# The gates of a gated recurrence: fewer passes over the squares, and all work in a new order

## The chip, the core and the metric

The kernel runs on one core of a Trainium2 chip. The metric is the device time of one execution in microseconds; the kernel before was timed three times, and the median counts. One further execution was recorded by the hardware profiler; all views of the profile are of that one. The engines are called TensorE (PE, with its weight loads as PEld), VectorE (DVE), ScalarE (ACT), GpSimd (POOL) and SyncE (SP, which only issues DMAs here).

## What is computed

A gated linear recurrence with complex gates over 768 steps, for 4 batches, 8 heads and a head size of 48, and behind it a low-rank token mixer with a two-layer network of channels (384 to 1536 to 384). Cut to what matters:

```python
mag = sqrt(a_re * a_re + a_im * a_im)
scale = minimum(mag, 0.999) / (mag + 1e-06)
a_re_n, a_im_n = a_re * scale, a_im * scale
for t in range(S):
    new_re = ar * S_re - ai * S_im
    new_im = ar * S_im + ai * S_re
    S_re, S_im = new_re + outer(k[t], v[t]), new_im
    y[t] = q[t] @ S_re

xt = x.transpose(0, 2, 1)                 # x: the y of all heads side by side
u = x + (xt @ U @ V).transpose(0, 2, 1)
out = u + maximum(u @ w_ch1, 0.0) @ w_ch2
```

All arrays are fp32 in effect; the weights of the mixer come as 64-bit floats and are converted in the kernel. The real parts of the gates lie between 0.85 and 0.95, the imaginary parts are normal with a spread of 0.1.

## The kernel before, in words

The tokens are cut into 24 chunks of 128 (six per batch), and two neighbouring chunks make a gate group, so there are 12 groups. Group 0 is worked on as two halves of one chunk each.

**Gates (the function `gates`).** The recurrence is not run step by step. The kernel takes the logarithm of each gate's magnitude and its angle, sums both along the chunk with a matmul against a triangular matrix, and uses the exponentials and the cosines and sines of these sums as weights of q and k. For that, `magnitudes_of` computes per group, on tiles of 128 tokens x 768 values (two chunks of 384):

- ScalarE squares both parts in one step of 1536 values, into the planes x and y.
- VectorE adds the squares and clips the sum into l (L655), puts the larger of the squares into x (L656), and runs two range tests on the parts themselves (L658), which tell whether the imaginary part anywhere exceeds the real part. Each test writes the maximum that it found into a column of the tile `bad` (an accumulator read).
- ScalarE takes Ln of l, then Exp with a scale of -0.5 and the bias log(1e-6) into y, then Ln(1 + y): this is the log of (mag + 1e-6)/mag.
- The clip at 0.999 is a step on VectorE in groups 0 to 2 (`SPREAD`, L666) and a Relu on ScalarE in the others. A VectorE step then completes the log of the gate in l (L445 in groups 0 to 2, L671 in the others). From group 3 on (`SPLIT`) l is split into two parts for faster matmuls (L677, L678).
- ScalarE takes Ln and Exp (scale -0.5) of x, which gives one over the larger part; VectorE multiplies it by the imaginary part. The arc tangent of that is the angle; it is taken later, under another activation table.

`within` sums l along the chunk (L692, L696) and takes the exponentials; `angles` and `waves` do the same for the angle. All activations are issued through the helper in L439.

**Chunks (`prep`, `chain`).** VectorE weighs q and k (L442), TensorE transposes them (L817), ScalarE copies the result (L823), and the matmuls of the chunk follow (L846, L866, L895, L903), with the state carried from chunk to chunk.

**Mixer (`mixer`).** For every two chunks there are the products with the weights: `up` (L992) and a corrected form of it for the first two chunks (L1032, with VectorE's L1038), `few` (L1104) and `down` (L1236). From mixer 2 on `few` does a Strassen-like scheme with 15 products, and from mixer 1 on `down_two` does a similar one; for that, differences of blocks of w2 are computed once (L617, L1306). The weights arrive as raw words over the SP queue and are converted by VectorE and ScalarE (L583 to L589).

**The order.** Every operation is registered with a planner (`Plan.add`) with its engine, an estimated cost, and what it reads and writes. The program is then emitted in the order of a fixed list, `ORDER`, of 2210 numbers. Each engine and each DMA queue executes its own part of the list strictly in order. `SPARE` says before which TensorE operations a number of idle 128x128 matmuls are put, to fill a wait.

**The check at the end (`judge`).** The columns of `bad` and the smallest of the exponentials are tested and counted. If anything is out of range, a general, step-by-step path (`in_general`) computes the whole result again.

## Time and profile before

| | |
|---|---|
| runs | 559.97, 560.68, 565.65 us |
| median | 560.68 us |
| span of the profiled execution | 559.4 us |
| ACT_TABLE_LOAD | 24, 30.8 us in all |
| HBM read and written | 33.60 MB and 4.76 MB |

The span runs from the first to the last instruction of the profiled execution; the times of the runs also hold what lies around it. The profiled execution's own time is its span and that frame; the runs stand between 0.6 and 6.2 us above the span, the median 1.3.

In a row of a group of instructions stand the line, the engine, the operation, the tiles written and read, the shape, the count, then the busy time, the mean duration in ns, and after the second bar the idle time of the engine just before these instructions with what ended it. In a row of waits stand the waiting engine with its tile and line, what it waited for, the sum in us, the number and the longest. In a row of a stretch of time stand its bounds and length, then the busy time of PE, PEld, DVE, ACT and POOL with the number of instructions, the granted TensorE clock as a share of full speed, the share of the 16 DMA engines, and GB/s. Line numbers are those of the kernel before; a line can be that of a helper through which many operations go, as L439 (activations), L442 (multiplications) and L445 (additions).

### The profile page before, as it was taken

The page shows a single profiled execution, that of the slowest core. Times are in us where ns is not written, and L with a number is a line of the kernel's source. Part 1 is how long each engine was busy: PE and PEld are TensorE (multiplying, and loading weights), DVE is VectorE, ACT ScalarE, POOL GpSimd, SP SyncE. Part 2 cuts the span into 40 slices and gives each one's busy share as a digit, 9 for nine tenths or more (in the row PEclk, how much of TensorE's full clock was granted, in tenths as well). Part 3 has the DMA queues.
Part 4 walks back from the last instruction along what each step waited for, and adds up shares of the span by engine and source line. Part 5 has one row for each costly group of instructions (what it writes and reads, how often), then busy time and mean ns, then how long its engine had stood idle before and what let it go on. Part 6 is the DMA issues. An engine that isn't in the chain of part 4 may idle for free.

```text
span 559.4 us, 16683 instructions
## 1 busy us (share of the span) xinstructions
PE 533.3 (95%) x7242; PEld 481.8 (86%) x7242; DVE 432.3 (77%) x828; ACT 317.7 (57%) x553; POOL 32.2 (6%) x61
## 2 busy tenths in 40 slices
PE   2899999989999999999999999999999999999996
PEld 1677786867799997999999997899999989999996
DVE  6999989899799998898896976977572726728352
ACT  6889999894657869576567855861323322111110
POOL 1000000000011000101001001001000000000000
PEclk9999999989999999999999999999999999999999
DMA  9969876331333254133342235020011000000001
GB/s 222 198 145 201 195 182 184 91 52 37 85 66 80 45 107 76 37 69 65 60 91 51 57 52 110 16 40 27 9 36 36 4 2 22 8 8 22 21 9 33
DMA packets 150687, 39.90 MB, mean 71 GB/s; under 512 B 145912, under 2 KB 147408, under 8 KB 150608
## 3 DMA queue, kind: packets, MB, share of 16 engines
q1 hardware_dynamic: 148400, 34.43, 31.2%
q0 software_dynamic: 2208, 4.35, 2.3%
q8 instruction: 58, 0.95, 0.7%
q14 instruction: 21, 0.17, 0.1%
HBM read 33.60 MB, written 4.76 MB: 69 GB/s over the span
## 4 chain that ended last, share of the span: by engine, by line
PE 53%; DVE 20%; issue 7%; ACT 4%; DMA 3%; POOL 0%; SPq 0%; DVEq 0%; ACTq 0%; POOLq 0%
PE down L1236 20%; PE few L1104 17%; PE dk L866 3%; PE tr L817 3%; ACT gate L439 2%; DMA gate<-F 2%; PE inner L846 2%; DVE xo L445 2%; PE y L903 2%; DVE QKC L442 2%; PE up L992 1%; DVE qk L442 1%; PE y L895 1%; DVE GS L751 1%; DVE GL L671 1%
## 5 line engine op out<-in xcount | busy, mean ns | idle before, releaser
L1112 ACT COPY h<-few 128x512 f32<-128x512 f32 x60 | 34.8, 584 | 86.0 <-PE few L1104 84.6
L439 ACT ACTIVATE gate<-gate 128x768 f32<-128x768 f32 (+2 forms) x74 | 65.9, 901 | 16.6 <-DVE GS L751 9.0
L1236 PE MATMUL down<-w,h 128*128 128x192 f32 x396 | 72.7, 330 | 0.2 <-DVE xo L445 0.2
L1236 PEld LDWEIGHTS down<-w,h 128*128 128x128 f32 x396 | 64.5, 190 | 2.7 <-DVE xo L445 1.1
L445 DVE TENSOR_TENSOR xo<-down,xo 128x192 f32<-128x192 f32 (+1 forms) x79 | 29.8, 386 | 41.9 <-PE down L1236 39.7
L823 ACT COPY QK<-tr 112x512 f32<-112x512 f32 x96 | 50.0, 596 | 20.3 <-PE tr L817 20.1
L1104 PE MATMUL few<-extra,w 128*128 128x128 f32 x400 | 50.2, 276 | 0.1
L1104 PEld LDWEIGHTS few<-extra,w 128*128 128x128 f32 x400 | 47.6, 192 | 0.7 <-PE mixed L961 0.4
L1116 DVE CUSTOM_DVE_ANT_1 h<-few,h 128x512 f32<-128x512 f32 x60 | 40.2, 686 | 8.1 <-PE few L1104 4.3
L442 DVE TENSOR_TENSOR QKC<-qk,cs 128x768 f32<-128x768 f32 x48 | 44.5, 952 | 0.8 <-PE tr L817 0.6
L445 DVE TENSOR_TENSOR h<-few,h 128x512 f32<-128x512 f32 x30 | 20.5, 687 | 23.8 <-PE few L1104 12.6
L1236 PE MATMUL down<-stage 128*128 128x192 f32 x198 | 38.0, 329 | 0.5 <-DVE xo L445 0.5
L1180 POOL DMA_DIRECT2D out_dram<-xo x32 | 18.1, 573 | 276.8 <-DVE xo L445 248.5
L1236 PEld LDWEIGHTS down<-stage 128*128 128x128 f32 x198 | 32.6, 190 | 1.7 <-DVE xo L445 1.4
L992 PE MATMUL up<-uT,w 128*128 128x256 f32 x144 | 32.4, 382 | 0.2 <-ACT uT L981 0.2
L1104 PE MATMUL few<-gate,w 128*128 128x128 f32 x240 | 31.8, 277 | 0.1
L817 PEld LDWEIGHTS tr<-ident,QKC 64*112 64x112 f32 x768 | 25.2, 135 | 7.5 <-DVE QKC L442 2.5
L436 ACT ACT_TABLE_LOAD x24 | 30.8, 1283 | 1.1 <-PEq L1440 0.7
L817 PE MATMUL tr<-ident,QKC 64*112 64x64 f32 x768 | 29.8, 226 | 1.4 <-DVE QKC L442 1.4
L992 PEld LDWEIGHTS up<-uT,w 128*128 128x128 f32 x144 | 27.0, 190 | 4.4 <-ACT uT L981 0.6
L1104 PEld LDWEIGHTS few<-gate,w 128*128 128x128 f32 x240 | 29.1, 192 | 0.3 <-PE few L1104 0.2
L439 ACT ACTIVATE cs<-F 128x384 f32<-128x384 f32 x48 | 24.1, 520 | 8.1 <-DVE F L765 7.9
(161 smaller groups left out, 1106.2 us busy)
## 6 DMA issues: line engine op xcount, KB each, us to landing
stage<-in_moe_w_ch_dram SPq DMA_DIRECT2D x12, 768.0 KB, 5.4
gate<-in_a_im_dram SPq DMA_DIRECT2D x24, 192.0 KB, 3.0
gate<-in_a_re_dram SPq DMA_DIRECT2D x24, 192.0 KB, 3.7
qk<-in_q_dram SPq DMA_DIRECT2D x24, 192.0 KB, 4.4
qk<-in_k_dram SPq DMA_DIRECT2D x24, 192.0 KB, 3.6
VP<-in_v_dram SPq DMA_DIRECT2D x24, 192.0 KB, 3.9
out_dram<-xo POOLq DMA_DIRECT2D x12, 192.0 KB, 2.2
out_dram<-xo POOLq DMA_DIRECT2D x20, 96.0 KB, 1.9
```

The lines of the kernel that those rows point to most:

```text
L436: ACT(1.37, rank, lambda: nc.scalar.preload_act_table_set(name), writes=[TABLE])
L439: return nc.scalar.activation(out=o, in_=i, func=f, **kw)
L442: nc.vector.tensor_tensor(out=o, in0=a, in1=b, op=OP.mult)
L445: nc.vector.tensor_tensor(out=o, in0=a, in1=b, op=OP.add)
L817: nc.tensor.transpose(out=get(*ps[r])[0:DQ, h], in_=get(*qkc)[at, h].rearrange("p u d -> p (u d)")[:, 0:DQ], identity=ident[at, at], tile_ ...
L823: nc.scalar.copy(out=get(*QK)[:, u].rearrange("p (h t) -> p h t", t=CH)[:, :, r * HC:(r + 1) * HC], in_=get(*ps[r])[0:DQ])
L992: nc.tensor.matmul(out=get(*ps)[:, e], lhsT=w1[:, f, (ff + e) * 128:(ff + e + 1) * 128], rhs=get(*uT)[:, f], start=(f == 0), stop=(f == KD ...
L1104: nc.tensor.matmul(out=get(*ps)[:, q], lhsT=w()[:, q * 128:(q + 1) * 128], rhs=v[0](), start=(n == 0 and q == 0), stop=True, skip_group_ch ...
L1112: ACT(c_act(n3 * CH) - 0.045, RU, lambda i=i, k=k: nc.scalar.copy(out=at(i, k), in_=get(*ps)), [ps], [o])
L1116: DVE(c_dve(n3 * CH), RU, lambda i=i, k=k: nc.vector._custom_dve(dve_ops.TENSOR_ADD_SAT, out=at(i, k), in0=get(*ps), in1=at(i, k), s0=math ...
L1180: queue.dma_start(out=out[b, c * CH:(c + 1) * CH, lo:hi], in_=get("xo", i)[:, lo:hi])
L1236: nc.tensor.matmul(out=get(*to)[:, part], lhsT=x(j), rhs=y[:, j], start=(first and j == 0), stop=(j == KH - 1), skip_group_check=not first)
```

## The change

1. ScalarE squares only the imaginary part, into y. The square of the real part is a VectorE step, max(a_re, 0) * a_re, into x.
2. The two range tests become one: max(y, 1e-30) >= x, counted into one column of `bad`.
3. The clipped sum of the squares goes into y in place, behind the test, which reads y before.
4. x now holds the square of the real part and no maximum, so the step of L656 goes. In groups 1 to 11 x and y lie side by side, and one Ln and one Exp of 1536 values each serve both. In group 0 they stay apart.
5. The factor 1e-6 moves from the bias of Exp to the scale of the next Ln. The clip step reads y and writes l, ahead of the Exp that overwrites y.
6. The product that reads a changed block of w2 now names that block's change as something it reads (`turned w2`), which the planner did not know before.
7. `ORDER` is another list, of 2175 numbers, and `SPARE` another table. Per group 1 to 11 three operations are gone, and one per half of group 0.

The operations of TensorE are the same 624 in number; the idle matmuls are 33 where they were 41. The core of the diff:

```diff
 ORDER = (
-    95, 93, 91, 94, 0, 92, 150, 5, 11, 96, 99, 149, 100, 152, 97, 3, 151, 4, 98, 101, 194, 115, 112, 2, 116, 102, 195, 113, 106, 104, 196, 117, 114,
...
+    0, 95, 91, 93, 96, 97, 98, 99, 94, 92, 5, 100, 101, 112, 111, 102, 103, 105, 106, 113, 114, 115, 104, 3, 190, 108, 7, 120, 116, 6, 8, 117, 11,
...
 SPARE = {
-    125: 2, 135: 9, 184: 1, 199: 21, 203: 1, 223: 2, 250: 3, 412: 2,
+    123: 2, 133: 5, 194: 8, 198: 11, 218: 6, 248: 1,
 }
...
-            def squares():
-                at, n = slice((lo - first) * DM, (hi - first) * DM), 4 if g < SINGLE and g % 2 else 2
-                act(GATE[:, 0:2, at], GATE[:, n:n + 2, at], AF.Square)
-            ACT(c_act(2 * W), R1, squares, AR + AI, [X] + Y)
-            DVE(cd, R1, lambda: nc.vector._custom_dve(dve_ops.TENSOR_ADD_SAT, out=t(l), in0=t(x), in1=t(y), s0=M2HI, s1=M2LO), [X] + Y, [L])
-            DVE(cd, R1, lambda: nc.vector.scalar_tensor_tensor(out=t(x), in0=t(x), scalar=M2LO, in1=t(y), op0=OP.max, op1=OP.max), Y, [X])
-            for u, o in enumerate((dve_ops.TENSOR_TENSOR_REDUCE_SUB_MAX, dve_ops.TENSOR_TENSOR_REDUCE_ADD_MAX)):
-                DVE(cd + 0.06, ("least", g), lambda u=u, o=o: nc.vector._custom_dve(
-                    o, out=low[:, 0:W], in0=t(ai), in1=t(ar), s0=-math.inf, s1=1.0 - 2.0 * u,
-                    accum_out=bad[:, 1 + 2 * lo + u:2 + 2 * lo + u]), AR + AI, [("low", 0), ("bad", 0, (lo, u))])
-            table(ca, R1, lambda: act(t(l), t(l), AF.Ln), [], [L])
-            table(ca + 0.09, R1, lambda: act(t(y), t(l), AF.Exp, scale=-0.5, bias=leps), [L], Y)
-            table(ca, R1, lambda: act(t(y), t(y), AF.Ln, bias=1.0), [], Y)
+            both = g > 0
+            def pair():
+                return GATE[:, 0:2, (lo - first) * DM:(hi - first) * DM]
+            ACT(ca, R1, lambda: act(t(y), t(ai), AF.Square), AI, Y)
+            DVE(cd, R1, lambda: nc.vector.scalar_tensor_tensor(out=t(x), in0=t(ar), scalar=0.0, in1=t(ar), op0=OP.max, op1=OP.mult), AR, [X])
+            DVE(cd + 0.06, R1, lambda: nc.vector.scalar_tensor_tensor(
+                out=low[:, 0:W], in0=t(y), scalar=M2LO, in1=t(x), op0=OP.max, op1=OP.is_ge, accum_out=bad[:, 1 + lo:2 + lo]),
+                Y + [X], [("low", 0), ("bad", 0, lo)])
+            DVE(cd, R1, lambda: nc.vector._custom_dve(dve_ops.TENSOR_ADD_SAT, out=t(y), in0=t(x), in1=t(y), s0=M2HI, s1=M2LO), [X], Y)
+            if both:
+                table(c_act(2 * W), R1, lambda: act(pair(), pair(), AF.Ln), [], [X] + Y)
+            else:
+                table(ca, R1, lambda: act(t(y), t(y), AF.Ln), [], Y)
             if on_dve:
-                DVE(c_one(W), R1, lambda: nc.vector.tensor_scalar(out=t(l), in0=t(l), scalar1=-0.5, scalar2=-LNMAX, op0=OP.mult, op1=OP.max), [], [L])
+                DVE(c_one(W), R1, lambda: nc.vector.tensor_scalar(out=t(l), in0=t(y), scalar1=-0.5, scalar2=-LNMAX, op0=OP.mult, op1=OP.max), Y, [L])
+            else:
+                ACT(ca + 0.09, R1, lambda: act(t(l), t(y), AF.Relu, scale=-0.5, bias=lmax), Y, [L])
+            if both:
+                table(c_act(2 * W), R1, lambda: act(pair(), pair(), AF.Exp, scale=-0.5), [], [X] + Y)
+            else:
+                table(ca, R1, lambda: act(t(y), t(y), AF.Exp, scale=-0.5), [], Y)
+            table(ca, R1, lambda: act(t(y), t(y), AF.Ln, scale=1e-6, bias=1.0), [], Y)
...
-            table(ca, R1, lambda: act(t(x), t(x), AF.Ln), [], [X])
-            table(ca, R1, lambda: act(t(x), t(x), AF.Exp, scale=-0.5), [], [X])
+            if not both:
+                table(ca, R1, lambda: act(t(x), t(x), AF.Ln), [], [X])
+                table(ca, R1, lambda: act(t(x), t(x), AF.Exp, scale=-0.5), [], [X])
             DVE(cd, R1, lambda: mul(t(x), t(x), t(ai)), AI, [X])
...
-            product(one, 0, lambda j: of(0, 1)[:, j], w2_of(0, 1), names, first=False)
+            product(one, 0, lambda j: of(0, 1)[:, j], w2_of(0, 1), lambda half: names(half) + [("turned w2", 0)], first=False)
...
-                                                                    op=OP.subtract), [("w2s", 0)], ALL_W2)
+                                                                    op=OP.subtract), [("w2s", 0)], ALL_W2 + [("turned w2", 0)])
```

## The prediction

> **What bounds the kernel now.** I read the page first, for the engines' shares and the clock.

> ```profile
> span 559.4 us, 16683 instructions
> ...
> PE 533.3 (95%) x7242; PEld 481.8 (86%) x7242; DVE 432.3 (77%) x828; ACT 317.7 (57%) x553; POOL 32.2 (6%) x61
> ...
> PEclk9999999989999999999999999999999999999999
> ```

> TensorE is busy for 95% of the span, but a matmul's end is modelled, so a waiting TensorE can look busy; the weight loads (PEld) tell more. The one slice with a lower digit in PEclk comes back below. Next I asked for busy time by stage, because shares over the whole span mix stages with different limits.

> ```profile
> 0.00:20.00 20.00, 7.54 (x31) 5.29 (x32) 14.66 (x38) 13.00 (x23) 2.30 (x14) 1.00 1.02 211
> 20.00:140.00 120.00, 113.82 (x1719) 88.67 (x1719) 111.98 (x183) 103.78 (x174) 2.47 (x3) 0.97 0.66 140
> 140.00:340.00 200.00, 199.34 (x2925) 184.99 (x2923) 177.37 (x338) 138.47 (x237) 16.70 (x26) 1.00 0.35 68
> 340.00:360.00 20.00, 18.27 (x475) 15.20 (x474) 14.10 (x28) 15.90 (x31) 0.97 (x2) 1.00 0.31 67
> ```

> The columns are length, PE, PEld, DVE, ACT, POOL, clock, DMA share, GB/s. There are two regimes. From 140 us on TensorE is the bound: it is idle 0.66 us in 200, and weight loads fill 185 of those 200. Before 140 us they fill 88.7 of 120, while VectorE fills 112 and ScalarE 104. In the middle of that stretch VectorE has no gap at all:

> ```profile
> 40.00:60.00 20.00, 19.38 (x283) 14.68 (x284) 20.00 (x32) 17.64 (x32) 0.00 (x0) 1.00 1.04 198
> ```

> So up to 140 us the pace is set by two elementwise queues that are nearly full, and after it by TensorE. The waits tell whether it is the queues' amount of work or the latency of a chain:

> ```profile
> PE es ps L696 <- DVE GL L445: 11.1, 1, 11.1
> ...
> DVE GL L671 <- ACT GL L439: 3.6, 1, 3.6
> ...
> PE up L1032 <- DVE extra L1038: 1.9, 2, 1.0
> ```

> The first row is TensorE's wait for the first gates at the start. The second is the longest wait of VectorE between 20 and 140 us, and the third the longest sum of TensorE there. Only once in 120 us did a gate's chain leave VectorE idle for long. The chain of waits shows the same (start, length, piece):

> ```profile
> 85.04 0.87 DVE GL L671
> ...
> 106.03 0.89 DVE w L589
> 106.91 0.88 DVE GL L655
> 107.81 0.84 ACT GL L439
> ...
> 140.60 0.97 DVE GL L655
> ...
> 317.59 0.96 DVE GL L671
> ```

> At 106.03 the gates' saturating sum (L655) stands behind a weight conversion on the same queue, not behind its own inputs. L655 at 106.91 is that of group 4 and at 140.60 that of group 5, so the gates of groups 0 to 4 lie before 140 us and seven groups after it. L671, the step that completes the log of a gate, stands in the chain five times, of which the first and the last are shown.

> **The change part by part.** The prices are means of the groups by form, 128x768 for groups 1 to 11 and 128x384 for each of the two halves of group 0:

> ```profile
> L658 DVE CUSTOM_DVE_ANT_0 low<-gate 128x768 f32<-128x768 f32 x22 | 20.9, 952 | 0.8 <-DMA gate<-in_a_im_dram 0.7
> ...
> L656 DVE SCALAR_TENSOR_TENSOR gate<-gate 128x768 f32<-128x768 f32 x11 | 10.4, 950 | 0.1
> ...
> L671 DVE SCALAR_TENSOR_TENSOR GL<-GL,gate 128x768 f32<-128x768 f32 x9 | 8.6, 956 | 5.3 <-ACT GL L439 4.3 <-ACT gate L439 1.0
> ...
> L658 DVE CUSTOM_DVE_ANT_0 low<-gate 128x384 f32<-128x384 f32 x4 | 2.2, 559 | 2.9 <-DMA gate<-in_a_re_dram 2.8
> L658 DVE DVE_READ_ACCUMULATOR2_ANT bad<- 128x1 f32 x26 | 2.2, 83 | 0.0
> ```

> VectorE, per group: before, the sum (L655), the maximum (L656) and two range tests (L658), each with an accumulator read of 83 ns. After, the square of the real part, one range test with one read, and the sum. One operation of 0.952 and one read of 0.083 go: 1.035 us. The square and the sum take the place of the maximum and the sum at the same size, with two fp32 operands as L656 has. In group 0 each half saves 0.559 + 0.083, together 1.28 us.

> ```profile
> L439 ACT ACTIVATE gate<-gate 128x768 f32<-128x768 f32 x55 | 45.7, 840 | 4.9 <-DMA gate<-in_a_re_dram 2.9 <-DVE gate L656 1.7
> ...
> L439 ACT ACTIVATE gate<-gate 128x1536 f32<-128x1536 f32 x11 | 16.4, 1487 | 11.7 <-DVE GS L751 9.0 <-issue 1.4 <-ACT xo L912 0.8
> ...
> L439 ACT ACTIVATE gate<-GL,leps 128x768 f32<-128x768 f32 x11 | 10.2, 930 | 1.1 <-DVE gate L656 1.1
> L439 ACT ACTIVATE GL<-GL 128x768 f32<-128x768 f32 x11 | 9.3, 844 | 3.4 <-DVE GL L655 3.2
> L439 ACT ACTIVATE GL<-GL,lmax 128x768 f32<-128x768 f32 x9 | 8.4, 933 | 0.0
> ...
> L439 ACT ACTIVATE gate<-gate 128x384 f32<-128x384 f32 x8 | 3.8, 512 | 0.0
> ...
> L439 ACT ACTIVATE gate<-GL,leps 128x384 f32<-128x384 f32 x2 | 1.2, 599 | 0.0
> L439 ACT ACTIVATE GL<-GL 128x384 f32<-128x384 f32 x2 | 1.0, 514 | 0.0
> ```

> ScalarE, groups 1 to 11: before, both squares in one step (1.487), Ln (0.844), Exp with a bias tile (0.930) and three more steps (3 x 0.840): 5.78 us. After, one square (0.840), Ln and Exp of both planes (2 x 1.487, the price of the 1536 form, whatever the function) and one Ln (0.840): 4.65 us. That saves 1.13 us. A half of group 0 goes from 0.840 + 0.514 + 0.599 + 3 x 0.512 = 3.49 to 6 x 0.512 = 3.07, so 0.84 us for both. The Relu (0.933) and the table loads stay.

> The only operation with no row is the range test as a plain scalar-tensor-tensor with an accumulator. Its nearest rows are the same operation without one (0.950) and the custom operation with one (0.952 + 0.083). I take 0.95 + 0.083. Less is excluded, since every two-operand fp32 step of this size lies at 0.95 or above; as the upper bound I take a second pass over the data for the accumulation, 0.95 us more per group and 0.56 per half. [...]

> Sum for the first regime: VectorE loses 1.28 + 4 x 1.035 = 5.4 us by 140 us, ScalarE 0.84 + 4 x 1.13 = 5.4. Both queues shrink alike, so neither takes over from the other, and what is late next is TensorE. I pass all 5.4 us on, since VectorE's 8 idle us in that stretch come from waits that the change leaves in place. TensorE can take it: it is idle 120 - 113.82 = 6.2 us there, and more is hidden in stretched matmuls. If TensorE's order left no room, nothing of it would pass.

> Second regime: seven groups save 7.2 us of VectorE and 7.9 of ScalarE, but TensorE's idle time is only 0.66 + 1.73 = 2.4 us between 140 and 360 us. I take 0.9 of it, between nothing and 2.4.

> The start: the new list puts the load of the prefix matrix ahead of the first gate loads on SP's queue, where it stood behind three of them.

> ```profile
> 0.73 0.44 SPq L542 DMA_DIRECT2D gate<-in_a_im_dram  x1
> ...
> 2.75 0.71 SPq L531 DMA_DIRECT2D prefix_z<-in_spans_dram  x1
> ```

> One issue of 0.71 us is thus moved ahead of everything. The first matmul waits 11.1 us on that path, so it costs between 0, if landing and not issue sets the data's time, and 0.7; I take 0.3. The fillers before waiting matmuls go from 41 to 33; they stand in waits and I give them nothing. In groups 0 to 2 the clipping step on VectorE now reads the plane that the next Exp overwrites, so that Exp waits for VectorE.

> ```profile
> L666 DVE TENSOR_SCALAR GL<-GL 128x384 f32<-128x384 f32 (+1 forms) x4 | 1.8, 454 | 0.0
> ```

> Four such steps take 1.8 us. Queued behind the Exp on ScalarE are the copies of transposed q and k; the new list puts four of those between the two steps of group 1 and a square or a log between those of each half of group 0, and they cover it. Uncovered it costs those 1.8 us. The added dependency of the w2 difference only restrains the planner and costs nothing. The remaining moves of the new list I can't price one by one; I allow 2.5 us either way.

> Together: -5.4 - 0.9 + 0.3 = -6.0 us on the span of 559.4, so 553.4. The runs are 559.97, 560.68 and 565.65; the median is 1.3 above the profiled span, which gives **554.7 us**, 552 to 557.5 with the allowance.

> **Rivals.** First, more gain: the half clock goes away.

> ```profile
> 120.32 1.93 PE L1032 MATMUL up<-V,more 32*128 32x256 f32 x6 [0.91 <-DVE extra L1038]
> ...
> 120.00:127.50 7.50, 6.98 (x120) 5.74 (x122) 7.50 (x10) 6.43 (x11) 0.77 (x1) 0.54 0.54 83
> ```

> Just before 120.32 us TensorE waits 0.91 us for L1038, half of its sum there, and in the 7.5 us from 120 on its clock is 0.54: 3.4 us of clock are lost. If a shorter VectorE queue ends these waits sooner, that comes on top: 551.3 us. [...]

> Second, no measurable change: the saved work leaves idle queues. For it: the DMA share is 1.02 and 1.04 up to 60 us, so loads may set the early pace, and only groups after that (two of the five before 140 us) would pay: about -2 us, 558.5. A range test with a second pass gives the same end: 2 x 0.56 + 4 x 0.95 = 4.9 us return and 559.6 is left. Against the loads: VectorE is busy 20.00 of 20 at 40 to 60 us, so data are there. Against the second pass: the custom step accumulates too, reads two planes too and takes 0.952. I give the loads 0.11 and the second pass 0.06.

> Third, **slower**: the chain of one gate gets longer and becomes the pace. Before: squares 1.487, sum 0.950, Ln 0.844, Exp 0.930, Ln 0.840, Relu 0.933, L671 0.956, together 6.9 us. After: square on VectorE 0.95, test 1.03 (it reads the plane that the sum overwrites, so it comes first), sum 0.95, Ln of both 1.487, Relu 0.933, Exp of both 1.487, Ln 0.840, L671 0.956, together 8.6: 1.7 us more. If L671 stands in the chain five times for its latency, and the shorter queues just idle, that is +8.5: 569 us. It decides from four such groups on (6.8 us). For it: the five rows of L671. Against it: the single wait of 3.6 us for ScalarE, and pieces like 106.03, where the queue ahead is what is late.

> Fourth, the test raises its flag and the general path runs: 768 steps of some ten operations on 576 elements, at about 0.7 us by L656's row, over 5 ms. The inputs speak against it: real parts from 0.85 to 0.95, imaginary parts with a spread of 0.1.

> **How the numbers follow.** Forecast 0.55, clock gain 0.15, no change 0.17 (0.11 and 0.06), slower 0.12, flag 0.01. About 1% is what a measurement of this kernel tells from none, so the edges are 555.1 and 566.3. The forecast's own range lies a little more than half below 555.1: 0.30 faster, 0.25 within. So faster 0.30 + 0.15 = 0.45, the same 0.25 + 0.17 = 0.42, slower 0.13. The range has to hold the clock gain and the unchanged case and reach some way to the slower one: 550 to 562.5.

> **What would show it.** Right: VectorE's sum falls by about 12.7 us and ScalarE's by 13 (5.4 + 7.2 and 5.4 + 7.9), the test has 950 ns a piece, five groups' gates are done by 135 us, and the weight loads' share of the first 135 us rises. The clock gain shows as a window without 0.54. Wrong: a test near 1.9 us; a wait of VectorE or TensorE for ScalarE's gates of more than 1 us in several groups; a first matmul later than 11.1 us; or a stage after 140 us in which TensorE idles more than 2.4 us, which would be the new order's doing.

## The result: slower by 0.85%, and the profile after

The changed kernel takes 566.34 us (median of 10 runs, 565.73 to 568.82). The kernel before, on the same chip, takes 561.03 us; one of its ten executions took 2982.67 us and is left out of the ratio. The ratio is 1.0085, with a 95% interval of 1.0062 to 1.0107. 554.7 us had been forecast. The profiled run took 567.48 us; its span is 565.6 us, 6.2 more than before, where the forecast had 6.0 less. From the page of the changed kernel:

```profile
span 565.6 us, 16573 instructions
PE 529.8 (94%) x7226; PEld 479.8 (85%) x7226; DVE 427.8 (76%) x801; ACT 309.7 (55%) x531; POOL 31.7 (6%) x61
...
PEclk9999999999999989999999999999999999999997
```

The page counts work that overlaps on one engine once. Added up record by record, VectorE went from 486.5 to 474.1 us and ScalarE from 350.8 to 337.5: 12.4 and 13.3 us less. So the work did go. The slice of PEclk with an 8 has moved from the ninth to the fifteenth, and a 7 stands in the last. Busy time by stage (length, PE, PEld, DVE, ACT, POOL, clock, DMA share, GB/s):

```profile
20.00:140.00 120.00, 113.75 (x1656) 87.04 (x1657) 110.82 (x168) 103.82 (x165) 2.47 (x3) 1.00 0.62 139
140.00:340.00 200.00, 196.21 (x3136) 183.40 (x3132) 169.90 (x317) 131.36 (x226) 14.71 (x23) 0.99 0.36 67
340.00:360.00 20.00, 19.81 (x307) 18.87 (x304) 15.32 (x35) 8.54 (x16) 2.73 (x4) 1.00 0.43 77
...
120.00:127.50 7.50, 7.50 (x134) 5.45 (x133) 6.34 (x11) 4.76 (x8) 0.41 (x1) 1.00 0.57 110
200.00:210.00 10.00, 8.68 (x246) 7.94 (x242) 7.95 (x13) 6.73 (x8) 0.00 (x0) 0.83 0.62 95
```

Up to 140 us TensorE is as busy as before (113.75 against 113.82). Between 140 and 340 us it idles 3.79 us, where it idled 0.66. The half clock at 120 to 127.5 us (0.50 for 6.83 us) is gone, and another one stands at 200 to 210 us (0.50 for 3.41 us). TensorE's waits, and those of SP's queue at the end:

```profile
PE es ps L702 <- DVE GL L443: 10.4, 1, 10.4
...
PE y L901 <- ACT GL L437: 1.3, 1, 1.3
```

```profile
SPq L1457 <- PEq L1457: 6.6, 2, 6.1
```

The first matmul comes at 10.4 us (11.1 before). The last row is new: in the closing barrier SP waits 6.1 us in one piece; before, its longest wait there was 1.3 us. The chain of waits ends like this (start, length, piece):

```profile
548.63 6.13 PE down L1242 x36
554.77 0.02 issue
554.79 0.36 DVE xo L443
555.15 0.07 DVE bad L1375
555.22 0.04 issue
555.26 0.20 PE bad ps L1382 x2
555.47 0.02 issue
555.49 0.14 DVE flag L1384
```

The last product ends at 554.75 us, against 554.51 before. The loss is behind it. In the list of before, the six steps of `judge` stand at places 1495 to 1890 of 2210, and the flag is written at 438.19 us. In the new list three of the six are the last three entries, and the flag is written at 555.63 us. Every engine reads the flag (L1402) before the branch (L1412), so GpSimd begins its closing steps only then. The records of GpSimd's own queue show start and length:

```
          before          after
flag      438.06 0.14     555.49 0.14
TENSOR_LOAD   542.50 0.49     555.67 0.69
INC_SWDGE_SEM 544.61 1.12     556.93 1.12
DRAIN         548.31 3.97     560.74 3.97
end of span   559.4           565.6
```

Before, these 10 us lay beneath TensorE's last matmuls. Now they lie behind them.

To see where the 6.2 us arose, I added up TensorE's steps of each list at the length that they have without a wait, and looked when each kernel has done the same sum. The lists differ in order, so equal sums are not the same steps, and single rows are good to some half a microsecond:

```
sum done, us      0     80     90    150    170    300    340    440   last matmul   span
before         11.1  113.9  129.8  192.7  213.6  348.2  391.2  494.3     554.5     559.4
after          10.4  114.0  125.0  189.7  215.3  347.9  388.6  493.2     555.5     565.6
judge early    10.6  114.5  125.5  190.1  216.0  348.5  389.2  494.1     555.9     561.1
short test      9.7  114.1  125.1  188.2  212.3  344.8  385.6  490.2     552.1     557.2
test twice     11.8  118.7  129.6  195.1  218.7  353.3  395.1  500.0     561.8     566.7
new in old     11.6  121.7  138.6  204.5  225.3  362.5  407.5  510.9     571.1     575.9
y later        10.5  113.9  125.4  190.1  213.5  346.1  386.8  491.8     553.6     558.4
```

The lower rows are experiments, told below. For the change: nothing is gained by 114 us and 4.8 us by 130, across the half clock of before. Of these 1.8 are gone by 190 us, and 4.7 more are lost by 214, where the wait of 1.3 us and the half clock lie. By 494 us TensorE is 1.1 us ahead again (before waits 1.6 us at 348), and at its last matmul, which is now the count's, it is 0.95 us late (0.24 at the last product). The other 5.2 us are the tail.

### The profile page after: what moved, and what is told of

It is laid out like the page before. It is cut to its first block, busy times and chain, and to the rows that moved or that the text cites. A ratio compares the mean times of both kernels' runs of the same rounds, so it can differ in the third digit from the quotient of the medians.

```text
span 565.6 us, 16573 instructions
## 1 busy us (share of the span) xinstructions
PE 529.8 (94%) x7226; PEld 479.8 (85%) x7226; DVE 427.8 (76%) x801; ACT 309.7 (55%) x531; POOL 31.7 (6%) x61
## 4 chain that ended last, share of the span: by engine, by line
PE 62%; DVE 15%; issue 10%; ACT 5%; DMA 3%; SPq 3%; POOL 0%; DVEq 0%; POOLq 0%; ACTq 0%
PE down L1242 22%; PE few L1110 21%; PE y L909 3%; PE tr L823 3%; PE inner L852 2%; ACT gate L437 2%; PE dk L872 2%; DMA gate<-F 2%; DVE QKC L440 2%; SPq L540 2%; PE y L901 2%; PE up L998 2%; PE uTp L983 1%; DVE xo L443 1%; PE mixed L967 1%
## 5 line engine op out<-in xcount | busy, mean ns | idle before, releaser
L437 ACT ACTIVATE gate<-gate 128x768 f32<-128x768 f32 (+2 forms) x78 | 75.1, 968 | 29.7 <-DVE gate L658 15.7
L1242 PE MATMUL down<-w,h 128*128 128x192 f32 x396 | 70.9, 328 | 1.1 <-DVE xo L443 1.0
L1110 PE MATMUL few<-extra,w 128*128 128x128 f32 x400 | 52.5, 278 | 1.0 <-DVE GM L443 0.8
L443 DVE TENSOR_TENSOR xo<-down,xo 128x192 f32<-128x192 f32 (+1 forms) x79 | 30.1, 385 | 29.1 <-PE down L1242 29.1
L1122 DVE CUSTOM_DVE_ANT_1 h<-few,h 128x512 f32<-128x512 f32 x60 | 39.8, 686 | 13.3 <-PE few L1110 9.1
L443 DVE TENSOR_TENSOR h<-few,h 128x512 f32<-128x512 f32 x30 | 20.5, 688 | 31.1 <-PE few L1110 15.9
L998 PE MATMUL up<-uT,w 128*128 128x256 f32 x144 | 34.2, 386 | 1.6 <-ACT h L437 1.2
L437 ACT ACTIVATE es<-es ps 128x384 f32<-128x384 f32 x48 | 21.1, 494 | 21.4 <-PE es ps L698 20.4
L1110 PE MATMUL few<-gate,w 128*128 128x128 f32 x240 | 32.2, 278 | 0.1
L1186 POOL DMA_DIRECT2D out_dram<-xo x32 | 20.1, 672 | 199.3 <-DVE xo L443 141.6
L823 PE MATMUL tr<-ident,QKC 64*112 64x64 f32 x768 | 28.1, 220 | 2.7 <-issue 0.9
```

The source lines that it names most:

```text
L437: return nc.scalar.activation(out=o, in_=i, func=f, **kw)
L443: nc.vector.tensor_tensor(out=o, in0=a, in1=b, op=OP.add)
L823: nc.tensor.transpose(out=get(*ps[r])[0:DQ, h], in_=get(*qkc)[at, h].rearrange("p u d -> p (u d)")[:, 0:DQ], identity=ident[at, at], tile_ ...
L998: nc.tensor.matmul(out=get(*ps)[:, e], lhsT=w1[:, f, (ff + e) * 128:(ff + e + 1) * 128], rhs=get(*uT)[:, f], start=(f == 0), stop=(f == KD ...
L1110: nc.tensor.matmul(out=get(*ps)[:, q], lhsT=w()[:, q * 128:(q + 1) * 128], rhs=v[0](), start=(n == 0 and q == 0), stop=True, skip_group_ch ...
L1122: DVE(c_dve(n3 * CH), RU, lambda i=i, k=k: nc.vector._custom_dve(dve_ops.TENSOR_ADD_SAT, out=at(i, k), in0=get(*ps), in1=at(i, k), s0=math ...
```

## The experiments

The kernels with a new list break it into other lines: code of L443 in the changed kernel stands at L432 in most of them, and all lines below shift by the same 10 to 12. Times are medians.

**The place of the count.** Three kernels move only the steps of `judge`: early in the new list, to the end of the old list, and two steps of TensorE ahead of the end of the new list.

```diff
-    1986, 2016, 1680, 1988, 1981, 1984, 1987, 2021, 2022, 1989,
+    1986, 2016, 1680, 2172, 1988, 1981, 1984, 1987, 2173, 2021, 2022, 2174, 1989,
...
-    2012, 1681, 2163, 2168, 2172, 2173, 2174,
+    2012, 1681, 2163, 2168,
```

> The changed kernel with the six steps of the range check's count moved from the end of the list to some 90% of it, about where the kernel before has them; nothing else moves. Theory: the flag that comes at 555.5 us sends GpSimd's closing work (load of the flag 0.69 us, 1.12 us, a drain of 3.97 us) behind the last matmul, while before it ended under the last matmuls. Then the span behind TensorE's last matmul falls from 10.1 to 4.9 us and the median from 566.3 to about 561.1. Rival: the last store or the closing barrier takes longer for another reason; then the time stays at 566.

Only three of the six steps stood at the end of the new list; these three are moved. Measured: 562.04 us; the kernel before 561.96; ratio 0.9999 (0.9964 to 1.0033).

```diff
-    2201, 2197, 2198, 2202, 2203,
+    2201, 2197, 2198, 2202, 2203, 2204, 2205, 2206, 2207, 2208, 2209,
...
```

> The kernel before with the six steps of the range check's count moved to the end of the list; nothing else moves. Theory of the late flag: 561.0 + 5.2 = 566.2 us, with a drain of GpSimd behind the last matmul. Rival (the end is longer for another reason): 561.

Measured: 567.72 us, ratio 1.0112 (1.0074 to 1.0149). The profiled execution took 570.46 us, 2.7 above the median. In it TensorE also ends 3.1 us later than in the kernel before, with a second half clock at 350 us; the tail behind the last product is 10.9 us.

```diff
-    2161, 2159, 2156, 2165, 2162, 2166, 2167, 2012, 1681, 2163, 2168, 2172, 2173, 2174,
+    2161, 2159, 2156, 2169, 2170, 2171, 2172, 2173, 2174, 2165, 2162, 2166, 2167, 2012, 1681, 2163, 2168,
...
```

> The changed kernel (566.3 us) with the count's steps ahead of TensorE's last two steps (0.96 us each) in the list, not behind them: the flag some 1.9 us earlier. If the end is the flag's time and 10 us, whatever TensorE does: 564.3 to 564.8 us. If only the very end of the list costs, because the flag then stands behind the last transfers: 561.5 to 562.5 us.

Measured: 563.95 us, ratio 1.0042 (1.0015 to 1.0068), a little under the range given; the flag came 2.8 us earlier, not 1.9. Its chain, its flag in the timeline, and SP's wait in the barrier:

```profile
552.49 0.12 PE bad ps L1370 x2
552.61 0.05 PE bad ps L1371 x2
552.66 2.16 PE down L1231 x12
```

```profile
552.70 0.14 DVE L1373 CAST flag<-bad ps 1x1 int32<-1x1 f32 x1 [0.94 <-PE bad ps L1371]
```

```profile
SPq L1446 <- PEq L1446: 4.2, 2, 3.6
```

The chain no longer ends with the flag, and yet the flag sets the end. Over the kernels (us):

```
                  flag     last product   end of span   end - flag   end - last product
before           438.19      554.51         559.40                         4.9
judge early      487.82      555.89         561.11                         5.2
y later          485.53      553.61         558.41                         4.8
two steps ahead  552.85      554.81         562.86         10.0            8.1
after            555.63      554.75         565.57          9.9           10.8
judge at the end 558.85      557.65         568.55          9.7           10.9
```

In these rows the end is the later of two: the last product and 4.8 to 5.2 us, or the flag and 9.7 to 10.0 us. In the three kernels with a late flag the span ends 0.86 us behind GpSimd's DRAIN of 3.97 us; in the eleven others it ends 6.7 to 7.2 us behind it. By these rows the flag has to be written about 5 us before the last product ends. With that restored, the change is worth nothing: the interval of the first kernel lies about 1. That leaves the question why 12 and 13 us less work on two engines gain nothing.

**Each gate in the other order.** One kernel runs the new gates in the list of before, with the steps that correspond at the same places; another runs the old gates in the new list, with the count early.

The first kernel against the changed one (new numbers of the same steps, in the places that they have before; the two squares where the double square stood, the test ahead of the sum, the clip behind the log):

```diff
 ORDER = (
-    0, 95, 91, 93, 96, 97, 98, 99, 94, 92, 5,
+    95, 93, 91, 94, 0, 92, 148, 5, 11, 96, 97,
...
 SPARE = {
-    123: 2, 133: 5, 194: 8, 198: 11, 218: 6, 248: 1,
+    123: 2, 133: 9, 179: 1, 194: 21, 198: 1, 218: 2, 245: 3, 404: 2,
```

> The changed gates in the order of the kernel before: each new step stands where its counterpart stood, the steps that are gone leave no gap, fillers as before, the count of the range check at about where it was. It shows the arithmetic alone. If the queues of VectorE and ScalarE set the pace up to 140 us, as the prediction had it, 5.4 us come off and the time is about 555.5. If their saved work only turns into idle time, 560 to 561. If the longer chain of a gate (1.7 us more) sets the pace, 563 or more.

Measured: 577.01 us, ratio 1.0262 (1.0228 to 1.0297): 15 us slower than the old gates in the same order. The second kernel, against the one before:

```diff
 ORDER = (
-    95, 93, 91, 94, 0, 92, 150, 5, 11, 96, 99,
+    0, 95, 91, 93, 96, 99, 100, 97, 98, 94, 92,
...
 SPARE = {
-    125: 2, 135: 9, 184: 1, 199: 21, 203: 1, 223: 2, 250: 3, 412: 2,
+    125: 2, 135: 5, 199: 8, 203: 11, 223: 6, 253: 1,
```

> The gates of before in the new order, the count of the range check early; the steps that the new list has no place for stand beside their neighbours. Against the run with the new gates, the new order and an early count it shows what the new gates are worth in the new order. If saved work is passed on there: 5 to 6 us slower than that run, about 567. If it turns into idle time: about 561 as well.

Measured: 575.98 us, ratio 1.0245 (1.0208 to 1.0283): 14 us slower than the new gates in the same order, 9 more than either reading had allowed. Each list suits its own gates; the steps that a list did not have were put beside their counterparts or neighbours, so a part of the 14 and 15 us may come of these places. The stage from 20 to 140 us, for the new gates in the old list and then the old gates in the new one:

```profile
20.00:140.00 120.00, 106.64 (x1691) 84.35 (x1692) 101.09 (x159) 98.98 (x163) 1.72 (x2) 0.96 0.64 140
```

```profile
20.00:140.00 120.00, 106.77 (x1605) 83.40 (x1605) 107.25 (x165) 101.17 (x167) 2.47 (x3) 0.97 0.60 137
```

In the first, VectorE is busy 11 us less than before (101.09 against 111.98), ScalarE 5 and TensorE 7: no queue is fuller than before, and all get on more slowly. A sum of work can't do that; steps that wait for each other can. TensorE's waits in this stage bear it out. Its longest after the one for L1038, in the kernel before, and its longest with the new gates in the old list:

```profile
PE ph L762 <- DVE F L765: 1.7, 3, 0.7
PE tr L817 <- DVE QKC L442: 1.4, 2, 1.2
```

```profile
PE tr L812 <- DVE QKC L429: 4.8, 4, 2.5
PE ph L757 <- DVE F L760: 2.8, 3, 1.5
PE up L1027 <- DVE extra L1033: 2.1, 2, 1.2
```

The waits for the weighted q and k (`QKC`) and for the angles (`F`), which the gates feed, grew by 3.4 and 1.1 us; TensorE's idle time grew by 7.2.

**What in the new gates the old order can't take.** The test reads the plane that the sum overwrites, so it stands between the squares and the sum; and log and exp of both planes take 1.49 us each where the chain needs one plane. Three kernels take these back in the old list: the test on one column alone, the pairs apart, and both.

```diff
-    out=low[:, 0:W], in0=t(y), scalar=M2LO, in1=t(x), op0=OP.max, op1=OP.is_ge, accum_out=bad[:, 1 + lo:2 + lo]),
+    out=low[:, 0:1], in0=t(y)[:, 0:1], scalar=M2LO, in1=t(x)[:, 0:1], op0=OP.max, op1=OP.is_ge, accum_out=bad[:, 1 + lo:2 + lo]),
```

> The new gates in the old order (577.0 us) with the test cut to one column. If the old order loses because a gate's chain is longer (the test stands between the squares and their sum), 0.85 us of some 3 that were added goes in each gate that TensorE waits for: 568 to 572 us. If it loses because the order of the queues no longer fits, whatever a step lasts: 575 us or more.

Measured: 570.27 us, ratio 1.0171 (1.0128 to 1.0214).

```diff
-    both = g > 0
+    both = False
...
```

> The new gates in the old order, but log and exp of the two squares as separate steps again, those of the second square at their old places; the one square and the one test stay. If the longer chain loses the 16 us, the pairs are the larger part of it (1.5 for 0.77 and 1.5 for 0.85 us, 1.4 a gate, against about 1 us for the test): 563 to 568 us. If the order's fit does: 574 us or more.

The list holds the 22 more steps, which is the rest of the edit. Measured: 570.54 us, ratio 1.0162 (1.0124 to 1.0199), 2.5 us above the range for the chain and 3.5 below that for the order's fit.

> The new gates in the old order with log and exp of the two squares separate and the test cut to one column (alone these gave 570.5 and 570.3 us, from 577.0). If the longer chain of a gate is what the old order could not take, both gains add: 563.5 to 565 us. If each lets the same wait go: 569 to 570 us.

Measured: 566.26 us, ratio 1.0068 (1.0034 to 1.0101). By the ratios the two take off 0.91% and 1.00% alone and 1.94% together: their gains add. By the medians they give 6.7 and 6.5 us alone and 10.7 together, 2.5 us short of the sum. Each interval is some 2 us wide either way, so whether part of the two lets the same waits go is not shown. Unpairing gives ScalarE more to do (four steps of 0.84 us for two of 1.49) and still gains, so it acts through the chain; the short test takes work and chain away at once. In this last profile, of the slowest of the ten executions (567.88 us), the half clock stands in two places (0.67 at 120 to 130 us and 0.78 at 350 to 360), which the kernel before has in one. So the longer chain of a gate is the likely reason for some two thirds of the loss in the old order, 10.7 of 15 us; the rest stays open.

**Less and more VectorE work in the new order.** Two kernels with the count early: the test on one column (the edit above), and the test issued twice.

```diff
-    DVE(cd + 0.06, R1, lambda: nc.vector.scalar_tensor_tensor(
+    DVE(cd + 0.06, R1, lambda: [nc.vector.scalar_tensor_tensor(
...
-        accum_out=bad[:, 1 + lo:2 + lo]),
+        accum_out=bad[:, 1 + lo:2 + lo]) for _ in range(2)],
```

> The changed kernel with the count's steps early (562.0 us), and the range test of each gate (957 ns, 13 of them) cut to one column of its 768 or 384, so that it counts almost nothing: about 0.85 us less VectorE work in each, 4 to 5 us of it before 140 us. If VectorE's sum sets the pace up to 140 us, as the prediction had it: 557 to 558 us. If TensorE waits only for single steps there and the sums have room: 561 to 562.5 us.

> The same kernel with each range test issued twice in a row: 0.95 us more VectorE work in each of 13 gates, and each gate's sum that much later. If VectorE's sum sets the pace up to 140 us: 567 us, 5 more than 562. If the sums have room: 562 to 564 us.

Measured: 558.75 us, ratio 0.9943 (0.9918 to 0.9968), with the short test; 568.89 us, ratio 1.0143 (1.0103 to 1.0183), with two. Taken alone, -3.3 and +6.9 us look like a pace set by VectorE's sum. The stage from 20 to 140 us says otherwise; the rows are those of the count early, of the short test and of the test twice:

```profile
20.00:140.00 120.00, 113.85 (x1642) 86.99 (x1642) 111.06 (x169) 104.33 (x167) 2.47 (x3) 1.00 0.62 139
```

```profile
20.00:140.00 120.00, 113.68 (x1668) 87.36 (x1666) 107.71 (x171) 103.54 (x166) 2.47 (x3) 1.00 0.63 139
```

```profile
20.00:140.00 120.00, 109.97 (x1623) 84.36 (x1622) 112.74 (x175) 100.48 (x164) 2.47 (x3) 1.00 0.63 140
```

3.35 us less on VectorE change nothing on TensorE (113.68 against 113.85). More work costs TensorE 3.9 us. In the table of sums the short test is 0.9 us ahead at the first matmul, 0.4 at 114 us, 1.9 at 190 and 3.7 at 214: half of its gain comes in the last stretch, where its profile has no half clock. The doubled test is 1.2 us behind at the first matmul, 4.2 at 114 and 5.0 at 190. So in the new list VectorE's steps have no time to spare, but shorter ones give TensorE next to nothing up to 114 us: what else it waits for is as late.

**The wait at 203 us.** In the kernel with the count early TensorE waits 1.59 us in the middle of a y product, put down to a step of ScalarE, and the clock halves for 3.4 us from 206.5 on (from 204.8 on in the changed kernel). One kernel moves this product behind the next steps of TensorE, another fills the wait with six spare matmuls.

```diff
-    909, 820, 907, 888, 886, 563, 1162, 1163, 860, 1164, 1165,
+    909, 820, 907, 886, 563, 1162, 1163, 860, 888, 1164, 1165,
```

> The changed kernel with the count's steps early (562.0 us), and one step of TensorE moved behind the next two of its list: the y product that waited 1.6 us at 203 us and behind which the granted clock fell to a half for 3.4 us. If the wait is for data and the half clock comes of the idle time: both go, 1.6 and 1.7 us, 558.5 to 559.5 us. If it is something that sits at that place whatever instruction stands there, or if later steps of TensorE are late anyway: 561 to 562.5 us.

Measured: 559.84 us, ratio 0.9973 (0.9951 to 0.9995), 0.3 us above the range for the idle time.

```diff
 SPARE = {
-    123: 2, 133: 5, 194: 8, 198: 11, 218: 6, 248: 1,
+    123: 2, 133: 5, 194: 8, 198: 11, 218: 6, 248: 1, 888: 6,
 }
```

> The same kernel with the y product left where it is, and six spare matmuls (192 ns of weight load each, some 1.5 us) issued into the time that TensorE waits ahead of it. If the half clock comes of the idle time: the wait stays, the clock stays full there, 560 to 560.5 us. If the clock falls for another reason: 562 us, or 563 if the spare matmuls delay the product.

Measured: 563.65 us, ratio 1.0046 (1.0020 to 1.0071). The timelines of the count early, of the product moved, and of the wait filled (start, length, step, count, idle time ahead of it):

```profile
201.21 2.06 PE L861 MATMUL dk<-VP,QKC 64*64 64x48 f32 x96
203.11 0.28 PE L890 MATMUL y<-VP,AT 64*64 64x48 f32 x2
204.98 0.68 PE L890 MATMUL y<-VP,AT 64*64 64x48 f32 x30 [1.59 <-ACT GL L426]
```

```profile
201.23 2.06 PE L861 MATMUL dk<-VP,QKC 64*64 64x48 f32 x96
203.22 0.59 PE L1231 MATMUL down<-stage 128*128 128x192 f32 x2
204.46 0.92 PE L1231 MATMUL down<-stage 128*128 128x192 f32 x4 [0.65 <-issue]
```

```profile
200.82 1.80 PE L861 MATMUL dk<-VP,QKC 64*48 64x48 f32 x78
202.55 0.46 PE L1383 MATMUL y<-ident 128*128 128x96 f32 x2
203.78 1.36 PE L1383 MATMUL y<-ident 128*128 128x96 f32 x10 [0.77 <-issue]
205.06 0.68 PE L890 MATMUL y<-VP,AT 64*64 64x48 f32 x32
```

Whatever stands behind the dk products, two matmuls of it run and then TensorE stops for 0.65 to 1.6 us. A `down` product and spare matmuls wait for no ScalarE there, and the profile names no releaser ("issue"). So the name in the first row misled: the stop belongs to the place in TensorE's stream, not to the y product's data. What it waits for there is told in the last section.

Both profiles have the clock at 1.00 between 200 and 210 us, but one profile each does not show that the half clock comes of the idle time. A half clock of 3.4 us takes 0.003 from an execution's mean clock (1.7 of some 560 us). Two of the six executions of the count early have a mean of 1.000, so with the same list it stays away at times. With the product moved none of ten executions lies under 0.998; with the wait filled three of ten lie at 0.992 to 0.995, so a half clock came in these, at this place or at another. Whether the idle time brings it is not settled.

Moving the product kept 2.3 us to the end of its profile, 1.7 of them the half clock. Filling gained nothing, and the forecast of 560 us for it was wrong: its profile is 0.8 us ahead at 208 us, but 0.65 of that stood before the filled place (the dk products start at 200.56 against 201.21 us), and its median is 1.6 us above that of the count early. The kernel with the product moved is faster than the kernel before by a bare 0.27%, and it is the fastest whole version found.

## Why the prediction was wrong

**The removed work was priced right.** VectorE lost 12.4 us by its records (12.7 forecast), ScalarE 13.3 (13). The new forms, by group:

```profile
L437 ACT ACTIVATE gate<-gate 128x1536 f32<-128x1536 f32 x22 | 32.8, 1491 | 14.8 <-DVE gate L658 14.5
...
L655 DVE SCALAR_TENSOR_TENSOR low<-gate 128x768 f32<-128x768 f32 x11 | 10.5, 957 | 1.1 <-ACT gate L437 0.5
...
L654 DVE SCALAR_TENSOR_TENSOR gate<-gate 128x768 f32<-128x768 f32 x11 | 10.5, 951 | 0.0
...
L655 DVE DVE_READ_ACCUMULATOR low<-gate 128x1 f32 x13 | 1.1, 83 | 0.0
```

The test with accumulation takes 957 ns and the read 83; the same operation without an accumulator (L654) takes 951. So there is no second pass: the forecast's upper bound of 0.95 us more a group was an assumption that no run shows.

**"I pass all 5.4 us on" failed.** TensorE is some 4 us ahead at 140 us, which looks close. But nothing of it was there at 114 us; it came where the kernel before has its half clock and its two waits for L1038, which is the first rival's mechanism. The step took two nearly full queues for the pace. In the new order, 3.35 us less on VectorE left TensorE's busy time as it was; in the old order, 11 us less came with 7 us less on TensorE. There TensorE waits for the ends of single chains, and the new gate's chain is longer, as the rival of the longer chain had it at a price of 8.5 us. Without the new order it came with a loss of 15 us. The last column of the first row above shows the chain, with ScalarE's paired logs waiting 14.5 us for VectorE's sum behind the test, but not its price: 12.9 us of ScalarE's waits for that sum lie behind 140 us, and only 1.5 between 20 and 140. With the new order and the count early, new gates and old come out alike. How the saved work and the longer chain cancel there is not shown step by step, and neither the forecast nor that rival had them cancel.

**"I take 0.9 of it" failed too.** From 140 us to the last matmul 5 us were lost instead. The prediction named the sign that came: a stage after 140 us in which TensorE idles more than 2.4 us. It idles 3.79 between 140 and 340 us. 1.3 of them and 1.7 of clock belong to the stop at 203 us. At the end of the list the new order has waits where the kernel before has none:

```profile
PE down L1242 <- DVE xo L443: 1.2, 2, 0.7
PE y L909 <- ACT xo L920: 0.6, 2, 0.3
PE bad ps L1382 <- DVE bad L1375: 0.4, 1, 0.4
```

These are rows from 430 to 560 us, 2.2 of the some 4 us lost behind 450 us or so; the rest I did not trace.

**"The remaining moves of the new list I can't price one by one; I allow 2.5 us either way" failed by the most.** One of those moves, of three small steps to the end of the list, costs 4.3 us (566.34 against 562.04; 4.8 by the ratios to the kernel before) and makes the change slower. The steps of `judge` have the last numbers in each list, and three of them end the new one. The trace of before has the flag at 438 us and GpSimd's closing steps beneath the last matmuls, so the cover that the move takes away could be read there. The prediction followed the moved load at the start and the fillers, and no step at the other end.

**What held.** The start: 10.4 us for the first matmul, under the 11.1 allowed. The general path is not taken. Of the signs of being right one failed: the weight loads of the first 135 us were to rise and fell, from 91.0 to 88.8 us. Another told nothing: five groups' gates by 135 us, since the fifth (group 4) has its L671 at 112.8 us in the kernel before already. The upper edge with the allowance is 557.2 us (554.7 and 2.5), not 557.5; nothing hangs on it. Without the moved count the forecast's second rival, no measurable change, would have been the result, though neither the loads nor a second pass was its reason.

On the span: forecast -6.0, measured +6.2. By the sums of TensorE's steps, 4.1 were gained by 140 us where 5.1 were forecast (1.0 missing), then some 5 lost where 0.9 was to be gained (6.0), then the tail with 5.2.

## What to carry to other kernels

When a list of all work is planned anew, follow the last entries first: what every engine must read before it can finish has to be written early enough that the slowest closing sequence, here GpSimd's 10 us, lies beneath other work. In this kernel less work on a nearly full queue was no gain where the step that others wait for did not end sooner; price the chain of one item and the sum of the queue apart, and test the claim by making one step shorter and one longer. Each of the two orders here loses 14 to 15 us of 560 with the other's gates, so arithmetic and order have to be judged together.

## What the hardware showed that I had not expected

**The closing sequence.** From the flag's write to the end of the span 9.7 to 10.0 us pass in the three kernels with a late flag, 3.97 of them in GpSimd's DRAIN. The DRAIN takes 3.97 us in all 14 profiles, also where GpSimd issued its last transfer 18 us before it (the count at the end of the old list, 545.7 and 563.7 us), so its length does not come of a transfer just issued.

**The stop at a place in the stream.** It comes in all eight kernels of the new order after the dk products (near 203 us; 208 with the test twice, 213 with the old gates), while loads hold the DMA engines at a share of 0.84 to 1.10 for 5 us. The page shows that instructions come by DMA as well:

```profile
q8 instruction: 59, 0.97, 0.7%
```

**The half clock is not a matter of the wait's length alone.** In the profiles, waits of 1.3 and 1.6 us there were followed by 3.4 us of half clock, and one of 1.4 us (the short test) and those of 1.1 us and less were not; and one and the same list (the count early) has executions with it (mean clock 0.994 in the profiled one) and without it (1.000 in two of six). The one at 120 us in the kernel before lasted 6.83 us, twice the 3.41 at 205 us in the changed kernel. What decides whether it comes is not shown.
